# V's columns into the padded tiles: copies on ScalarE in place of transfers, weight pieces behind the fillers

## The chip, the cores and the metric

The kernel runs as one program on one core of a Trainium2 chip. The metric is the device time of one execution in microseconds. A core has TensorE (PE; PEld is its weight load), VectorE (DVE), ScalarE (ACT), GpSimd (POOL) and SyncE (SP), which issues the plain DMAs from one queue, in program order. Each engine runs its own instructions in order and waits for semaphores of the others.

## The reference

Two stages. The first is attention over pooled keys for 8 batches, 8 heads, 576 queries and head size 64: keys and values are averaged over groups of 8, which leaves 72 per head.

```
k_p = k.reshape(B, H, 72, 8, D).mean(axis=3)
v_p = v.reshape(B, H, 72, 8, D).mean(axis=3)
scores = scale * q @ k_p^T ;  scores -= max
attn = exp(scores) / (sum(exp(scores)) + 1e-9)
x = attn @ v_p                      # then (B*S, H*D) = (4608, 512)
```

The second is a top-1 mixture of 8 experts: for each of the 4608 rows the expert with the largest `x @ w_gate`, then `relu(x @ w1[e]) @ w2[e]`, times the gate's probability.

## The kernel before

**Two parts.** The attention part works through 36 units of 128 query rows, all 8 heads at a time. Four units belong to each batch, and one more per pair of batches holds the last 64 rows of both; so units 0 to 3 are batch 0, 4 to 7 batch 1, 8 their remainder, 9 to 12 batch 2 and so on. Each unit also computes the gate's logits, and after every group of units a chain on VectorE (the routing chain) finds each row's expert and place; rows are then scattered to memory by expert. The second part loads blocks of 256 rows of an expert and multiplies them with the expert's weights, which are split into two halves of 16 bits (high and low).

**One unit** (the loop at the end of the attention part). TensorE transposes the probabilities (`u_pt`, tile `pp`), ScalarE casts them to 16 bits (`ph`, L519), VectorE makes the remainder (`pl`, L525), and TensorE forms the weighted sum with V (`u_pv`, L552, tile `po`). VectorE then scales it (`u_nrm`, `ri`, L582 to L590). In between stand the scores of later units (`g_s`, L493), their row minimum (`g_min`) and eight exponentials on ScalarE (`g_exp`, L510), the transposes of later queries (`g_qt`, L470, and their copy L473), and "fillers": pieces of the routing chain and of V's preparation that are taken from a list, up to five behind `u_pv`. A filler's ranking matmul (`rank`, L656) stands in TensorE's order and waits for the routing chain on VectorE (L632, L638, L643, L647).

**V's padded tile.** The 576 pooled rows of a batch (72 for each of 8 heads) lie in 5 chunks of 128 rows, so a chunk holds rows of two or three heads. The weighted sum needs for each chunk and head a block of 72 columns (64 of V, 8 of V times the gate's weights) in which rows of other heads are zero: `VB`, three tiles used in turn, 128 rows x (high, low) x 5 chunks x 3 slots x 74 columns. A batch has 12 such blocks. The compact V columns are in `vc`, made by GpSimd's pooling, ScalarE and VectorE; the last step on VectorE is the filler `value` (L396). Batch 0 is masked by VectorE (`masked`). For batches 1 to 7 the tile is set to zero once, and 12 small transfers from SBUF to SBUF put each head's rows into their block: `value` appends them to the list `moves`, and the loop issues up to 12 of them a unit (units 0 to 3) or 6 (later) on SyncE's queue, behind the unit's other loads (`run(i, "sp")`). One more kind of move, `bd<-bd`, copies a batch's prepared K block to the other half of the partitions.

**Order.** The order is written out by hand: `put(unit, position, function)` places work at a position of a unit, and the loop runs the positions in sequence. Loads of K, V, q and weights stand at position `sp`; ScalarE's high halves of the first expert's weights at `act2`; quarters of three low halves (`lsplit`, L836) at `dve`, which on VectorE lies ahead of the fillers. GpSimd's pooling additions (L330, L332) are made to start behind VectorE's reciprocal of a unit.

Of the kernel before, what the change touches and what calls it, by code (L numbers as in the profile page):

```python
# [12 lines left out]
AF = mybir.ActivationFunctionType  # L13
# [13 lines left out]
HS = (0, 1, 3, 5, 5)  # L27
SLOTS = ((0, 2), (0, 3), (0, 3), (0, 3), (2, 3))
# [3 lines left out]
def kernel(  # L32
# [10 lines left out]
    nc = tc.nc  # L43
    B, H, S, D = q.shape
    N, Dm = out.shape
    E = w1.shape[0]
    F = w1.shape[2]
    KP = S // POOL
# [90 lines left out]
    mk = consts.tile([128, 5, 3], F32, name="mk")  # L139
# [79 lines left out]
    VB = [loads.tile([128, 2, 5, 3, CS], F16, name=f"vb{i}") for i in range(3)]  # L219
# [63 lines left out]
        nc.gpsimd.memset(BD[i], 0.0)  # L283

    def blank(i):
        nc.gpsimd.memset(VB[i] if i else VB[i][:, 1, :, :, 72:73], 0.0)
        nc.gpsimd.tensor_tensor(VB[i][:, 0, :, :, 72:73], mk16[:, :, :, None], z16[:, :, :, None], op=OP.add)

    for i in range(3):
        blank(i)  # L290
# [4 lines left out]
    KVS = {}  # L295
    fillers = []
    moves = []

    TWO = {"away", "best", "onehot", "guard", "value", "<lambda>", "early_int", "early_shift", "again", "again_int"}

    def fill(n=1, one=False):
        while n and fillers and not fillers[0][1] and not (one and fillers[0][2].__name__ in TWO):
            fillers.pop(0)[2]()
            n -= 1
# [8 lines left out]
    def fill_pe():  # L313
        if fillers and fillers[0][1]:
            fillers.pop(0)[2]()
# [78 lines left out]
    def v_dve(b):  # L394
        vp, vc = KVS.pop(("vp", b)), KVS["vc", b]
        nc.vector.scalar_tensor_tensor(vc[:, 1, :, 0:D], vp, SV, vc[:, 0, :, 0:D], op0=OP.mult, op1=OP.subtract)  # L396
# [9 lines left out]
    def u_dve(b):  # L406
        pm, vc = KVS.pop(("pu", b)), KVS["vc", b]
        Z = {}

        def cross():  # L410
            Z["ut"] = work.tile([128, 5, 3, E], F32, name="ut", bufs=1)
            nc.vector.tensor_tensor(Z["ut"], pm[:, 0:120].rearrange("p (c s e) -> p c s e", s=3, e=E),
                                    mk[:, :, :, None].to_broadcast([128, 5, 3, E]), op=OP.mult)

        def gather():
            Z["u"] = pm[:, 128:128 + 5 * E].rearrange("p (c e) -> p c e", e=E)
            nc.vector.tensor_reduce(Z["u"], Z["ut"].rearrange("p c s e -> p c e s"), axis=AX.X, op=OP.add)

        def high():
            nc.vector.tensor_scalar(vc[:, 0, :, D:], Z["u"], SV, None, op0=OP.mult)  # L420

        def low():
            nc.vector.scalar_tensor_tensor(vc[:, 1, :, D:], Z["u"], SV, vc[:, 0, :, D:], op0=OP.mult,
                                           op1=OP.subtract)

        def value():
            v_dve(b)
            if b > 0:
                KVS.pop(("vc", b))
                for c in range(5):  # L430
                    for s in range(*SLOTS[c]):
                        h = HS[c] + s
                        r0, r1 = max(KP * h, 128 * c) - 128 * c, min(KP * h + KP, 128 * c + 128) - 128 * c
                        moves.append((VB[b % 3][r0:r1, :, c, s, 0:D + E], vc[r0:r1, :, c, :], b))

        first = [cross, gather, high, low, value]
        if b < 1:
            first += [lambda: masked(b, 0), lambda: masked(b, 1)]
        fillers[0:0] = [(-1, False, f) for f in first]

    def masked(b, s):
        vc = KVS["vc", b] if s == 0 else KVS.pop(("vc", b))
        nc.vector.tensor_tensor(VB[b][:, s, :, :, 0:D + E], vc[:, s, :, None, :].to_broadcast([128, 5, 3, D + E]),
                                mk16[:, :, :, None].to_broadcast([128, 5, 3, D + E]), op=OP.mult)
# [61 lines left out]
    def g_exp(G, j):  # L506
        ps, nmx, slots = PS_.pop((G, j))
        for x, (h, s) in enumerate(slots):
            p = pbuf[groups[G][s] % 4]
            nc.scalar.activation(p[:, h * KP:(h + 1) * KP], ps[:, x * KP:(x + 1) * KP], AF.Exp,  # L510
                                 bias=nmx[:, x:x + 1], scale=-1.0)

    def u_pt(i):
        p = pbuf[i % 4]
        pp = psA.tile([128, 1024], F32, name="pp")
        for c in range(5):
            nc.tensor.transpose(pp[:, c * 128:(c + 1) * 128], p[:, c * 128:(c + 1) * 128], ident)  # L517
        ph = work.tile([128, 640], F16, name="ph")
        nc.scalar.activation(ph, pp[:, 0:640], AF.Copy, scale=SP)  # L519
        PP_[i] = (pp, ph)  # L520

    def u_lo(i):
        pp, ph = PP_[i]
        pl = work.tile([128, 640], F16, name="pl")
        nc.vector.scalar_tensor_tensor(pl, pp[:, 0:640], SP, ph, op0=OP.mult, op1=OP.subtract)  # L525
        PP_[i] = (ph, pl)

    def u_pv(i):
        b, r = units[i]
        ph, pl = PP_.pop(i)  # L530
        assert all(m[2] > b + (r is None) for m in moves)
        po = psA.tile([128, 2, 512], F32, name="po")
        PO_[i] = po
        first = {}
        for x, y in ((0, 0), (0, 1), (1, 0)):
            a = (ph, pl)[x]
            for c in range(5):
                h0, hend = HS[c] + SLOTS[c][0], HS[c] + SLOTS[c][1]
                while h0 < hend:
                    half = h0 // 4  # L540
                    h1 = min(hend, 4 * half + 4)
                    sl = slice(h0 - HS[c], h1 - HS[c])
                    cols = slice((h0 - 4 * half) * CW, (h1 - 4 * half) * CW)
                    st = first.get(half, True)
                    if r is None:
                        for s in range(2):
                            nc.tensor.matmul(po[64 * s:64 * s + 64, half, cols],
                                             a[:, c * 128 + 64 * s:c * 128 + 64 * s + 64],
                                             VB[(b + s) % 3][:, y, c, sl, 0:CW], start=st, stop=False,
                                             skip_group_check=True)  # L550
                    else:
                        nc.tensor.matmul(po[:, half, cols], a[:, c * 128:(c + 1) * 128],  # L552
                                         VB[b % 3][:, y, c, sl, 0:CW], start=st, stop=False, skip_group_check=True)
                    first[half] = False
                    h0 = h1
# [39 lines left out]
    def flush(n=99, upto=99):  # L595
        while n and pend and pend[0][0] <= upto:
            _, f, u = pend.pop(0)
            f(u)
            n -= 1
# [147 lines left out]
    for c in (4, 2, 3, 0, 1):  # L747
        n = 128 if c < 4 else 64
# [41 lines left out]
    def put(i, pos, f, *a):  # L790
        assert 0 <= i < NU
        hooks.setdefault((i, pos), []).append((f, a))
# [14 lines left out]
    for g in range(NPAIR):  # L807
        u0 = 9 * g
        e, o = 2 * g, 2 * g + 1
        if g:  # L810
            for b, at, last in ((e, u0 - 11, u0 - 8), (o, u0 - 7, u0 - 3)):
                first = 1 if (g == 1 and b == e) else 0
                for f, x in ((pool_k, 0), (pool_v, 2)):
                    for y in range(2):
                        put(POOLAT[b] + x + y, "q", f, b, y)
                    n = 2 * b + x // 2 + 3
# [24 lines left out]
        put(at, "q", wsplit, 0, j, "p", 0, on_beat)  # L841
    for j, at in ((1, 15), (3, 23), (4, 27)):
        for x in range(4):
            put(at + x, "dve", lsplit, j, x, 4)

    def pass_ids(g, i, h, j):
        nc.gpsimd.tensor_tensor(g, h, zf.to_broadcast([128, 2]), op=OP.add)
# [69 lines left out]
    def run(i, pos):  # L917
        for f, a in hooks.pop((i, pos), []):
            f(*a)

    def routes(i):
        gidx, u = GOF[i]
        if u == bounds[gidx][1] - 1:
            return route(gidx)
# [34 lines left out]
    for i in range(NU):  # L959
        A, Z = halves.get(2 * i), halves.get(2 * i + 1)  # L960
        Y = halves.get(2 * i - 1)
        if i < 30 and aged:
            flush(1)
            run(i, "q")
        else:
            run(i, "q")
            flush(1)
        u_pt(i)
        if A:
            g_s(*A)  # L970
        if Y:
            g_exp(*Y)
        if i in turns:
            g_qt(*turns[i])
        if (i, "pe") not in hooks:
            fill_pe()
        run(i, "pe")
        u_lo(i)
        if A:
            g_min(*A)  # L980
            g_exp(*A)
        run(i, "act")
        run(i, "dve")
        u_pv(i)
        fill(5 if i < 30 else 4)
        run(i, "pe2")
        fill_pe()
        run(i, "sp")
        for _ in range(min(12 if i < 4 else 6, len(moves))):
            nc.sync.dma_start(*moves.pop(0)[:2])  # L990
        if Z:
            g_s(*Z)
        aged = len(pend)
        u_nrm(i, (lambda: g_min(*Z)) if Z else None)
        run(i, "act2")
        run(i, "dve2")
        last = routes(i)
        fill(3 if i >= NU - 3 else 2, POOLAT[2] < i < 30)
# [323 lines left out]
```

## Time and profile before

| | us |
|---|---|
| median of 3 runs | 646.71 (644.49 to 648.65) |
| profiled execution, its own time | 643.21 |
| its span, first to last instruction | 641.4 |
| busy: TensorE, VectorE, ScalarE, GpSimd | 582.9, 324.4, 279.9, 266.9 |
| mean granted TensorE clock | 0.946 |

The profile is of one execution that was not among the three timed ones. Busy time of an engine counts overlapping instructions once. The granted clock is told as a share of 2.4 GHz; 0.50 is the 1.2 GHz level.

### The profile page before, as it was taken

The numbers are of one execution on the slowest core, as the hardware profiler recorded it, in microseconds if no ns is written. First come the engines' busy times: TensorE is split into PE (matmuls) and PEld (weight loads), VectorE is DVE, ScalarE is ACT, GpSimd is POOL, SyncE is SP. The second block draws the span as 40 slices with busy tenths as digits, with TensorE's granted clock in tenths as the row PEclk, the third lists the DMA queues.
The fourth block names the chain that finished last, engine by engine and source line by source line (L and its number), as shares of the span: only waits on it lengthen the run. The fifth ranks groups of instructions, "written<-read, shape, count | busy, mean of one in ns | idle before, by whom it ended". The sixth has DMA issues, their size and how long they took to land. (4 is left out here: it accounts for less than half of the span.)

```text
span 641.4 us, 15846 instructions
## 1 busy us (share of the span) xinstructions
PE 582.9 (91%) x4631; PEld 432.6 (67%) x4632; DVE 324.4 (51%) x736; ACT 279.9 (44%) x628; POOL 266.9 (42%) x477
## 2 busy tenths in 40 slices
PE   6897869789868989899999999999999999999983
PEld 4796758779767746666776667677667677667661
DVE  5565929967788664512551122146122731273672
ACT  1584829865766323421542222235222721262671
POOL 7583828677886351320432111223203132214264
PEclk7597969977879999999999999999999999999998
DMA  8974787886725469496467222334823283318310
GB/s 249 301 259 108 212 243 213 248 245 189 222 79 116 165 168 329 116 411 210 98 208 250 65 49 66 98 79 128 306 52 87 58 306 111 93 33 299 75 42 11
DMA packets 105417, 105.78 MB, mean 165 GB/s; under 512 B 63523, under 2 KB 73763, under 8 KB 105381
## 3 DMA queue, kind: packets, MB, share of 16 engines
q1 hardware_dynamic: 98740, 85.62, 47.6%
q0 software_dynamic: 6640, 19.71, 8.2%
q8 instruction: 18, 0.29, 0.2%
q14 instruction: 19, 0.15, 0.1%
HBM read 71.77 MB, written 22.06 MB: 146 GB/s over the span
## 5 line engine op out<-in xcount | busy, mean ns | idle before, releaser
L1020 PEld LDWEIGHTS <-bd 128*128 128x128 f16 x936 | 91.1, 98 | 108.7 <-DVE bd L1014 2.2
L1014 DVE SCALAR_TENSOR_TENSOR bd<-ps,bd 128x512 f16<-128x512 f32 (+1 forms) x44 | 27.4, 630 | 145.3 <-ACT bd L1010 127.6
L1230 POOL TENSOR_TENSOR spacer<-ql,iG 1x1 f32<-1x1 f32 x44 | 17.9, 406 | 165.9 <-ACT ql L1226 151.8
L510 ACT ACTIVATE both<-ps,nmx 128x72 f32<-128x72 f32 x288 | 68.6, 326 | 9.0 <-DVE nmx L503 8.7
L1020 PE MATMUL po<-kv,bd 128*128 128x512 f16 x264 | 59.0, 379 | 2.5 <-ACT bd L1010 1.8
L1020 PE MATMUL po<-w,bd 128*128 128x512 f16 x264 | 59.1, 379 | 0.0
L493 PE MATMUL ps<-bd,qT 128*128 128x144 f32 x256 | 53.4, 342 | 5.3 <-DMA bd<-bd 3.9
L1231 POOL DMA_INDIRECT out_dram<-ql,iG x44 | 48.5, 1102 | 21.7 <-issue 20.0
L1010 ACT ACTIVATE bd<-ps 128x512 f16<-128x512 f32 (+1 forms) x44 | 23.8, 547 | 67.2 <-PE L946 33.4
L330 POOL TENSOR_TENSOR st<-kv 128x1280 f32<-128x1280 f32 x14 | 40.9, 2921 | 22.7 <-DVE ri L583 14.6
L1020 PE MATMUL pq<-kv,bd 128*128 128x512 f16 x216 | 48.1, 379 | 0.0
L493 PEld LDWEIGHTS ps<-bd,qT 128*128 128x128 f32 x256 | 42.8, 228 | 6.9 <-issue 4.3
L519 ACT ACTIVATE ph<-pp 128x640 f16<-128x640 f32 x36 | 25.4, 704 | 49.8 <-PE pp L517 47.4
L552 PE MATMUL po<-vb,ph 128*128 128x146 f16 (+2 forms) x384 | 34.8, 241 | 12.6 <-DMA vb<-vc 7.9
L685 POOL DMA_INDIRECT x_by_expert<-both,rpos x36 | 35.5, 987 | 25.4 <-DVE both L681 5.5
L946 PE MATMUL ps<-kv,w 128*128 128x256 f16 (+1 forms) x176 | 43.1, 258 | 3.3 <-ACT kv L111 2.0
L948 PE MATMUL ps<-kv,qt 128*128 128x256 f16 (+1 forms) x176 | 44.8, 263 | 1.0 <-DVE qt L113 1.0
L946 PE MATMUL ps<-kv,qt 128*128 128x256 f16 (+1 forms) x176 | 44.8, 263 | 0.0
L947 PE MATMUL ps<-kv,qt 128*128 128x256 f16 (+1 forms) x176 | 44.8, 263 | 0.0
L948 PE MATMUL ps<-kv,w 128*128 128x256 f16 (+1 forms) x176 | 43.1, 258 | 0.0
L947 PE MATMUL ps<-kv,w 128*128 128x256 f16 (+1 forms) x176 | 43.1, 258 | 0.0
L1020 PE MATMUL pq<-w,bd 128*128 128x512 f16 x192 | 42.7, 379 | 0.0
(250 smaller groups left out, 1354.8 us busy)
## 6 DMA issues: line engine op xcount, KB each, us to landing
st<-in_moe_w_dram SPq DMA_DIRECT2D x8, 2048.0 KB
both<-in_moe_w_dram SPq DMA_DIRECT2D x6, 2048.0 KB, 10.4
vb<-x_by_expert SPq DMA_DIRECT2D x16, 514.0 KB
kv<-in_k_dram SPq DMA_DIRECT2D x7, 1024.0 KB
kv<-in_v_dram SPq DMA_DIRECT2D x7, 1024.0 KB
qt<-in_q_dram SPq DMA_DIRECT2D x6, 1024.0 KB
st<-in_moe_w_dram SPq DMA_DIRECT2D x4, 1024.0 KB
qt<-in_q_dram SPq DMA_DIRECT2D x4, 512.0 KB
```

The source lines that it names most:

```text
L330: on_beat(nc.gpsimd.tensor_tensor(t1, src[:, :, 0:4 * D], src[:, :, 4 * D:], op=OP.add))
L493: nc.tensor.matmul(ps[:, x * 2 * KP:(x + 1) * 2 * KP], t[:, h, :], BD[b % 3][:, :, h, :], start=True, stop=True)
L510: nc.scalar.activation(p[:, h * KP:(h + 1) * KP], ps[:, x * KP:(x + 1) * KP], AF.Exp, bias=nmx[:, x:x + 1], scale=-1.0)
L519: nc.scalar.activation(ph, pp[:, 0:640], AF.Copy, scale=SP)
L552: nc.tensor.matmul(po[:, half, cols], a[:, c * 128:(c + 1) * 128], VB[b % 3][:, y, c, sl, 0:CW], start=st, stop=False, skip_group_check=True)
L685: st = nc.gpsimd.indirect_dma_start(out=xs, out_offset=bass.IndirectOffsetOnAxis(ap=Z["pos"][:, u:u + 1], axis=0), in_=X[:, u, :], in_offs ...
L946: nc.tensor.matmul(dst, wh, xT[:, d, 0:n], start=(d == 0), stop=False)
L947: nc.tensor.matmul(dst, wh, xT[:, DC + d, 0:n], start=False, stop=False)
L948: nc.tensor.matmul(dst, wl, xT[:, d, 0:n], start=False, stop=(d == DC - 1))
L1014: V.scalar_tensor_tensor(l, p, 0.0, h, op0=OP.max, op1=OP.subtract)
L1020: nc.tensor.matmul(y, hT[x][:, f, 128 * j:128 * j + 128], W2[s][z][:, f, :], start=(half == x == z == f == 0), stop=(half == z == 1 and f ...
L1231: st = nc.gpsimd.indirect_dma_start(out=out, out_offset=bass.IndirectOffsetOnAxis(ap=iG[:, j:j + 1], axis=0), in_=ys[j], in_offset=None, b ...
```

## The change

Batches 1 to 7: the 12 transfers of a batch are gone. In their place ScalarE copies whole 128-row blocks of `vc` into the padded tile, each scaled by a column of `mk` that is one in the head's rows and zero in the others (`place`). `value` lists the 12 blocks, and the loop issues up to 6 copies (units 0 to 3) or 4 (later) a unit, behind `act2`. Since the copies write the zeros too, only one column of the tiles is still cleared at the start. The moves that are left (`bd<-bd`) are issued as soon as they are listed. The quarters of the weights' low halves go to a new position `dve3`, behind the fillers.

```diff
     def blank(i):
-        nc.gpsimd.memset(VB[i] if i else VB[i][:, 1, :, :, 72:73], 0.0)
+        nc.gpsimd.memset(VB[i][:, 1, :, :, 72:73], 0.0)
...
         def value():
             v_dve(b)
             if b > 0:
-                KVS.pop(("vc", b))
-                for c in range(5):
-                    for s in range(*SLOTS[c]):
-                        h = HS[c] + s
-                        r0, r1 = max(KP * h, 128 * c) - 128 * c, min(KP * h + KP, 128 * c + 128) - 128 * c
-                        moves.append((VB[b % 3][r0:r1, :, c, s, 0:D + E], vc[r0:r1, :, c, :], b))
+                places.extend((b, c, s) for c in range(5) for s in range(*SLOTS[c]))
...
+    def place(n):
+        for b, c, s in places[:n]:
+            nc.scalar.activation(VB[b % 3][:, :, c, s, 0:D + E], KVS["vc", b][:, :, c, :], AF.Copy,
+                                 scale=mk[:, c, s:s + 1])
+        del places[:n]
...
     for j, at in ((1, 15), (3, 23), (4, 27)):
         for x in range(4):
-            put(at + x, "dve", lsplit, j, x, 4)
+            put(at + x, "dve3", lsplit, j, x, 4)
...
         fill(5 if i < 30 else 4)
+        run(i, "dve3")
         run(i, "pe2")
         fill_pe()
         run(i, "sp")
-        for _ in range(min(12 if i < 4 else 6, len(moves))):
+        for _ in range(len(moves)):
             nc.sync.dma_start(*moves.pop(0)[:2])
...
         run(i, "act2")
+        place(6 if i < 4 else 4)
         run(i, "dve2")
```

ScalarE's order in units 2 and 3, behind the copy of batch 2's K block (`bd_171`); `vb_173` is batch 1's padded tile. Before:

```order
L368 ACTIVATE bd_171<-pq 64x512
L519 ACTIVATE ph<-pp 128x640
L510 ACTIVATE both<-ps,nmx 128x72 x4
L473 ACTIVATE qT<-pq 128x512
L510 ACTIVATE both<-ps,nmx 128x72 x4
```

And now (lines behind the edit are numbered two or three higher):

```order
L369 ACTIVATE bd_171<-pq 64x512
L439 ACTIVATE vb_173<-vc,mk 128x2x72 x6
L521 ACTIVATE ph<-pp 128x640
L512 ACTIVATE both<-ps,nmx 128x72 x4
L475 ACTIVATE qT<-pq 128x512
L512 ACTIVATE both<-ps,nmx 128x72 x4
L439 ACTIVATE vb_173<-vc,mk 128x2x72 x6
```

Six copies stand ahead of unit 3's cast `ph`, and six more ahead of unit 4's.

SyncE's queue in units 7 to 9: `vb_174` is batch 2's padded tile, `bd_169` batch 3's K block, `st_64` a weight load. Before:

```order
L990 DMA vb_174<-vc 24x2x72
L990 DMA vb_174<-vc 48x2x72
L990 DMA vb_174<-vc 72x2x72
L990 DMA vb_174<-vc 8x2x72
L990 DMA vb_174<-vc 64x2x72
L247 DMA kv_163<-in_k_dram 64x512
L250 DMA kv_163<-in_k_dram 128x4x512
L990 DMA bd_169<-bd_169 64x576
L99 DMA st_64<-in_moe_w_dram 128x2x1024
```

And now:

```order
L254 DMA qt_166<-in_q_dram 128x8x256
L247 DMA kv_150<-in_v_dram 64x512
L250 DMA kv_150<-in_v_dram 128x4x512
L247 DMA kv_163<-in_k_dram 64x512
L250 DMA kv_163<-in_k_dram 128x4x512
L993 DMA bd_169<-bd_169 64x576
L99 DMA st_64<-in_moe_w_dram 128x2x1024
```

The K load and the block's copy directly follow the loads of q and V; the small transfers are gone.

VectorE's order in unit 16, from the remainder `pl` on; `w_01_61<-st_64` is the weight piece, `ra`, `req`, `rm`, `oh` the routing chain. Before:

```order
L525 SCALAR_TENSOR_TENSOR pl<-pp,ph 128x640
L503 TENSOR_REDUCE nmx<-ps 128x4
L836 SCALAR_TENSOR_TENSOR w_01_61<-st_64,w_00_60 128x256
L632 TENSOR_TENSOR ra<-L,rm 128x32
L638 SCALAR_TENSOR_TENSOR req<-ra,down 128x32
L643 TENSOR_REDUCE rm_1797<-req 128x4
L647 TENSOR_TENSOR oh<-req,rm_1797 128x32
L582 TENSOR_SCALAR ri<-po 128x8
```

And now:

```order
L527 SCALAR_TENSOR_TENSOR pl<-pp,ph 128x640
L505 TENSOR_REDUCE nmx<-ps 128x4
L634 TENSOR_TENSOR ra<-L,rm 128x32
L640 SCALAR_TENSOR_TENSOR req<-ra,down 128x32
L645 TENSOR_REDUCE rm_1796<-req 128x4
L649 TENSOR_TENSOR oh<-req,rm_1796 128x32
L838 SCALAR_TENSOR_TENSOR w_01_61<-st_64,w_00_60 128x256
L584 TENSOR_SCALAR ri<-po 128x8
```

The piece has moved from ahead of the routing chain to behind it, still ahead of the scaling. Units 24 and 28 have the same picture.

## Rows read from the trace of the kernel before

**Rows 1.** Stretches (us): length, busy PE, PEld, DVE, ACT, POOL, clock, DMA share, GB/s.

```profile
0.00:219.40 219.40, 178.81 (x1621) 159.07 (x1623) 155.37 (x480) 129.74 (x421) 146.72 (x177) 0.85 0.72 207
219.40:641.40 422.00, 404.13 (x3013) 273.53 (x3010) 169.07 (x257) 150.17 (x207) 120.17 (x300) 0.99 0.48 143
54.00:58.00 4.00, 3.22 (x24) 2.84 (x24) 1.09 (x4) 0.00 (x0) 0.61 (x1) 0.50 0.61 150
76.00:96.00 20.00, 12.42 (x88) 11.13 (x87) 8.11 (x29) 6.37 (x21) 7.54 (x8) 0.74 0.90 264
126.00:136.00 10.00, 8.19 (x50) 7.83 (x51) 5.92 (x19) 5.04 (x16) 3.40 (x3) 0.66 0.95 278
```

**Rows 2.** Waits, 30 to 219.4 us: who for whom, total us, times, longest.

```profile
ACT ph L519 <- PE pp L517: 47.4, 26, 7.0
...
PE po L552 <- DMA vb<-vc: 7.9, 6, 2.0
...
PE ps L493 <- DMA bd<-bd: 3.9, 1, 3.9
...
ACT w L111 <- DMA st<-in_moe_w_dram: 1.8, 1, 1.8
```

**Rows 3.** TensorE's timeline in unit 4: start, us, instruction, [idle before].

```profile
51.98 0.24 PE L552 MATMUL po<-vb,ph 128*128 128x146 f16 x1 [1.46 <-DMA vb<-vc]
54.18 0.34 PE L552 MATMUL po<-vb,ph 128*128 128x219 f16 x1 [1.96 <-DMA vb<-vc]
55.12 0.95 PE L552 MATMUL po<-vb,ph 128*128 128x73 f16 x7 [0.60 <-DMA vb<-vc]
```

**Rows 4.** SyncE's timeline, 38 to 122 us: issues.

```profile
44.02 9.80 SPq L990 DMA_DIRECT2D vb<-vc  x12
...
80.78 0.51 SPq L990 DMA_DIRECT2D bd<-bd  x1
...
114.92 4.93 SPq L990 DMA_DIRECT2D vb<-vc  x6
119.94 0.54 SPq L254 DMA_DIRECT2D qt<-in_q_dram  x1
```

**Rows 5.** TensorE's timeline, units 9, 10 and 18.

```profile
80.68 0.30 PE L552 MATMUL po<-vb,ph 128*128 128x146 f16 x1 [2.03 <-DMA vb<-vc]
82.59 1.16 PE L552 MATMUL po<-vb,ph 128*128 128x219 f16 x8 [1.61 <-DMA vb<-vc]
...
85.39 1.27 PE L517 MATMUL pp<-ident,both 128*128 128x128 f32 x5
90.60 1.30 PE L493 MATMUL ps<-bd,qT 128*128 128x144 f32 x4 [3.94 <-DMA bd<-bd]
...
127.81 1.02 PE L470 MATMUL pq<-ident,qt 128*128 128x128 f32 x4 [1.96 <-DMA qt<-in_q_dram]
```

**Rows 6.** ScalarE's groups, 30 to 219.4 us: count, busy us, mean ns, idle before.

```profile
L510 ACT ACTIVATE both<-ps,nmx 128x72 f32<-128x72 f32 x271 | 64.7, 326 | 4.3 <-DVE nmx L503 4.0
...
L111 ACT ACTIVATE w<-st 128x1024 f16<-128x1024 f32 x8 | 8.6, 1072 | 1.8 <-DMA st<-in_moe_w_dram 1.8
...
L392 ACT ACTIVATE vc<-vp 128x320 f16<-128x320 f32 x7 | 3.3, 474 | 0.0
```

**Rows 7.** ScalarE's timeline in units 3 and 4.

```profile
45.05 0.70 ACT L519 ACTIVATE ph<-pp 128x640 f16<-128x640 f32 x1 [0.51 <-PE pp L517]
45.65 0.95 ACT L510 ACTIVATE both<-ps,nmx 128x72 f32<-128x72 f32 x4
...
48.45 0.70 ACT L519 ACTIVATE ph<-pp 128x640 f16<-128x640 f32 x1 [0.48 <-PE pp L517]
```

**Rows 8.** VectorE's timeline in units 16 and 20.

```profile
118.35 1.20 DVE L836 SCALAR_TENSOR_TENSOR w<-st,w 128x256 f16<-128x256 f32 x1
...
140.38 2.81 DVE L632 TENSOR_TENSOR ra<-L,rm 128x32 f32<-128x32 f32 x1
```

**Rows 9.** GpSimd's timeline in unit 20.

```profile
140.22 2.90 POOL L330 TENSOR_TENSOR st<-kv 128x1280 f32<-128x1280 f32 x1
```

More of the change, by code (lines that the diff above doesn't have):

```diff
@@ L297 @@
     moves = []
+    places = []
     TWO = {"away", "best", "onehot", "guard", "value", "<lambda>", "early_int", "early_shift", "again", "again_int"}
@@ L530, in u_pv @@
         ph, pl = PP_.pop(i)
-        assert all(m[2] > b + (r is None) for m in moves)
+        assert all(x > b + (r is None) for x, *_ in places) and all(m[2] > b + (r is None) for m in moves)
         po = psA.tile([128, 2, 512], F32, name="po")
```

## The prediction, made before the result was known

> **What bounds the kernel now.** I read the busy time by stage first [rows 1]. Up to 219.4 us, where the last attention unit ends, TensorE is busy for 178.8 us at a mean granted clock of 0.85; the 422 us behind it run at 0.99 with 404 us busy. The edit touches only the first part, and what it moves in the second begins a little earlier or later as a whole, so all terms below are of these 219 us. The list of waits [rows 2] says who holds the first part up. ScalarE waits 47.4 us, over 26 units, for TensorE's transposes: it is not the bound as a whole. TensorE waits 7.9 us for the small transfers that write V into the padded tile, 3.9 us for the copy of K's block, and ScalarE once 1.8 us for a weight load.
>
> Then the single places. In unit 4 the weighted sum stops for 1.46, 1.96 and 0.60 us, each time for the next small transfer [rows 3]. The SyncE timeline shows why [rows 4]: the twelve transfers of batch 1 could not start before 44.02, took 9.80 us to issue (0.82 us each), and stood in front of everything else. In unit 9 the same wait is 2.03 and 1.61 us [rows 5], and 3.94 us follow for K's block of batch 3, whose copy was issued only at 80.78 [rows 4, 5]. In unit 18 the transposes wait 1.96 us for a q load that was issued at 119.94, right behind six small transfers begun at 114.92 [rows 4, 5].
>
> A stop costs more than itself: after the stops in unit 4 the granted clock is 0.50, the 1.2 GHz level, at 54 to 58 us; it is 0.74 over 76 to 96 and 0.66 over 126 to 136 [rows 1]. Each time one of these stops stood just ahead of it.
>
> **The change, term by term**, against the profiled execution's own 643.2 us.
>
> *Unit 4.* The waits end: 7.9 less 3.64 of unit 9 is 4.3 us [rows 2, 5]. TensorE then runs some 4 us of the path at half clock, which costs 2.0 us. Gain 6.3; bounds 4.3 (the clock falls anyway) and 6.3.
>
> *Unit 9.* 2.03 and 1.61 are 3.64 us. From 82.59 to the end of the transposes at 85.39 + 1.27 = 86.66, 4.1 us are run at the low level: 2.0 more. Gain 5.6, bounds 3.6 and 5.6.
>
> *Unit 10, K's block.* In SyncE's order six small transfers disappear ahead of the K load and the block copy, so the load can be issued when its buffer is free and the copy when ScalarE has written the block (unit 8), about 6 us earlier than 80.78. The copy then has only that load in front of it; but TensorE arrives 5 us earlier too, and DMA is already busy for 0.90 of 76 to 96 us [rows 1]. Bounds 0 and 3.94 + 2.0 of low clock = 5.9. I take 5.0, nearer to the upper end, because q's load and the load of V issue before the copy and land in the stretch that is now spent on issuing.
>
> *Unit 18.* The q load is in SyncE's program at unit 15; without the six transfers before it (4.93 us) it issues 5 us earlier, against a wait of 1.96. With the clock, (1 − 0.66) × 10 = 3.4 us, the upper bound is 5.4, the lower 0. VectorE has dense work in this unit, so I take 4.0.
>
> *The weight load.* SyncE had twelve transfers around it; ScalarE's 1.8 us for it [rows 2] should go. Bounds 0 and 1.8; taken 1.8.
>
> *ScalarE's copies.* 84 copies of 128 x 144 are new, a shape and operand pattern that no row shows together. Below: four exponentials with a column as operand take 0.95 us [rows 7] and one alone 0.326 [rows 6], so they follow each other at (0.95 − 0.326) / 3 = 0.21 us; 72 more elements at (1072 − 474) / (1024 − 320) = 0.85 ns [rows 6] add 0.06. One copy every 0.27 us: 84 × 0.27 = 22.7 us, 3.2 per batch. Above: if copies did not overlap, the 0.326 us of the exponential [rows 6] plus 0.06 is 0.39 us, 33 in all. I take 22.7, as the exponentials do overlap. The Trainium skill (ScalarE: Activation LUTs, What ACT_TABLE_LOAD costs) gives 186 ns + 0.833 ns an element, 93 ns more for a pointer operand, and an overlap of 93 ns: an estimate of 0.31 us a copy, 25.7 us in all, by which the exposed part below would be 9 us rather than 8.
>
> What of it is exposed is a matter of the unit's pace. A plain unit takes 48.45 − 45.05 = 3.40 us, and ScalarE is idle for 0.48 of them [rows 7]; four copies need 1.07, six 1.6. So units 2 and 3 lose about 1.1 each (2.2), and the next three batches, placed beside units of about this pace, 3.2 less three times 0.5, that is about 1.5 each (4.5). The last three lie in units that other work stretches to 5 to 9 us: 0.5 each (1.5). Behind the copies on ScalarE stands the cast of the next unit's probabilities, for which VectorE's low part and the weighted sum wait. Cost 8; bounds 0 (all in the 47.4 us of waiting) and 33 (all exposed).
>
> *Weight pieces behind the fillers.* In units 16, 24 and 28 a piece stood before the routing chain on which the ranking matmul waits; the longest shown here took 1.20 us [rows 8]. If that came back in each of the three units, the gain would be 3.6. But the routing chain's own first subtraction took 2.81 us in unit 20 without a piece before it, while GpSimd's addition ran from 140.22 to 143.12 [rows 8, 9], so the wait can pass from the piece to the subtraction. Gain 0.5, bounds 0 and 3.6. The Trainium skill (SBUF — State Buffer, Who interferes with whom) says that a VectorE instruction with two SBUF inputs contends with a GpSimd instruction that reads SBUF and that the later one blocks; piece and subtraction both have two. By it the term is near 0, without it 3.6; the 2.81 us agrees with it.
>
> *The rest.* The smaller memsets lie beside the first loads: nothing; without that cover they would still be a gain. SyncE's later waits and the landing of small transfers leave with them.
>
> *What is late next.* VectorE and GpSimd: when units follow more closely, GpSimd's additions meet VectorE's chain more often. I charge one more stop like the 2.81 us.
>
> Sum: −(6.3 + 5.6 + 5.0 + 4.0 + 1.8 + 0.5) + 8 + 2.8 = −12.4. Against 643.2 that is 630.8; the three timed runs before have a median of 646.7, 3.5 above the profiled execution, and 646.7 − 12.4 = 634.3. I forecast **633 us**.
>
> **Rivals.**
>
> *The waits only change their name.* K's block still comes late, because the loads that issue earlier fill the queue in front of it (DMA busy 0.90 in 76 to 96 speaks for that), and the copies are exposed for 12 us. Then 6.3 + 5.6 + 2.0 + 1.8 − 12 − 2.8 leaves 1 us: about 646, no change. Against it: the queue moved little while SyncE was issuing, 0.61 at 54 to 58.
>
> *ScalarE becomes the bound.* Its place is the cast at the head of each of the 20 units with copies. It decides once four copies cost more than the idle 0.48 us and nothing later in the unit absorbs the rest: at 0.39 us each, 33 us exposed less 23.2 gained is 10 us slower, 656. For it speaks that the exponentials already fill most of the 3.40 us; against it that they overlap, and that ScalarE waits 47.4 us for TensorE. The Trainium skill (ScalarE: Activation LUTs, Rules for kernel authors) advises VectorE rather than ScalarE for simple elementwise work, which fits this case; here VectorE has no room either (unit 16 is dense with it).
>
> *More comes back than I count.* The upper bounds of all gains, 28.6, and a cost of 5 give 646.7 − 23.6 = 623.
>
> That the change does something else is excluded: the orders show 84 copies on ScalarE and none of the small transfers left on SyncE.
>
> **Chances.** The forecast (626 to 641) 0.62, waits that change their name (641 to 651) 0.19, ScalarE as the bound 0.09, more than counted 0.10. About 1%, 6.5 us, is what a measurement of this kernel can tell from no change, and the forecast's lower edge touches it: faster 0.74, same 0.17, slower 0.09. The range runs from 623 (all upper bounds) to 645 (the first rival taken in nearly whole).
>
> **What would show it.** In the profile of the changed kernel: no wait of the weighted sum for a DMA in units 4 and 9, and a granted clock near 1.00 at the places that now show 0.50; K's block landed before unit 10 asks for it; the q load of unit 18 issued 5 us or more ahead; copies one every 0.27 us; TensorE's waits for the cast longer than now, by 8 us in all; the attention stage over at about 207 us, and the part behind it as long as before. I am wrong if the stage ends after 215 us: then either the block copy or the copies' exposure is what I mis-sized.

## The result, and the profile after

The changed kernel takes **620.5 us** (median of 4 runs, 619.44 to 622.84) where the kernel before, run beside it, takes 647.68 (4 runs, 644.49 to 648.7): ratio 0.9623, 95% interval 0.9558 to 0.9687. On another chip it was 620.53 against 643.81, ratio 0.9632 (0.959 to 0.9674). The forecast was 633, so the sign was right and the gain about twice the forecast; the time lies 2.5 us below the range (623 to 645), and below the 623 of the third rival. The profiled execution took 622.84 us, span 618.7, mean granted clock 0.967.

By stretch (columns as in [rows 1]), the changed kernel's attention stage now ends at 197.1 us (start of the last unit's scaling on VectorE; 219.2 before), 22.1 earlier; the part behind it is as long as before, 421.4 against 422.0. The last three are units 3 and 4, 8 to 12, and 17 and 18:

```profile
0.00:197.30 197.30, 167.08 (x1624) 147.49 (x1626) 148.99 (x480) 152.72 (x505) 143.91 (x177) 0.91 0.76 224
197.30:618.70 421.40, 404.08 (x3009) 273.07 (x3007) 169.36 (x257) 150.06 (x207) 118.90 (x300) 0.99 0.48 143
50.00:54.00 4.00, 2.79 (x35) 2.18 (x33) 2.73 (x11) 4.00 (x16) 2.13 (x1) 1.00 0.00 0
72.00:92.00 20.00, 18.30 (x185) 16.83 (x184) 16.11 (x56) 19.12 (x66) 17.10 (x18) 1.00 0.87 256
108.00:118.00 10.00, 9.27 (x109) 8.56 (x107) 9.26 (x33) 9.11 (x28) 7.60 (x8) 1.00 1.03 316
```

The places that ran at a granted clock of 0.50, 0.74 and 0.66 run at 1.00. DMA is as busy as before (0.87 to 1.03): the transfers that stay did not have to become fewer.

The list of waits, 24 to 197.3 us (who for whom, total us, times, longest), answers to [rows 2]. No wait of TensorE for a DMA is left; ScalarE's wait for the transposes fell from 47.4 to 11.9:

```profile
DVE pl L527 <- ACT ph L521: 17.6, 22, 1.4
...
ACT ph L521 <- PE pp L519: 11.9, 12, 2.4
...
PE po L554 <- ACT ph L521: 7.9, 10, 1.2
...
PE pq L658 <- DVE oh L649: 6.2, 8, 2.0
```

TensorE's timeline in units 4, 9, 10 and 18 answers to [rows 3, 5]. The weighted sums run through, the scores of unit 10 (79.47) and the transposes of unit 18 (112.19) wait for nothing; what is left in unit 4 is 0.65 us for the cast behind the copies and 0.57 for the routing chain:

```profile
51.84 0.96 PE L554 MATMUL po<-vb,ph 128*128 128x146 f16 x12 [0.65 <-ACT ph L521]
52.70 0.57 PE L554 MATMUL po<-vb,pl 128*128 128x146 f16 x6
53.84 0.19 PE L658 MATMUL pq<-oh,before 128*128 128x32 f16 x1 [0.57 <-DVE oh L649]
...
74.29 0.96 PE L554 MATMUL po<-vb,ph 128*128 128x146 f16 x12
...
79.47 0.73 PE L495 MATMUL ps<-bd,qT 128*128 128x144 f32 x4
...
112.19 0.60 PE L472 MATMUL pq<-ident,qt 128*128 128x128 f32 x4
```

SyncE's timeline (issues) answers to [rows 4]:

```profile
62.57 0.58 SPq L250 DMA_DIRECT2D kv<-in_k_dram  x1
71.55 0.48 SPq L993 DMA_DIRECT2D bd<-bd  x1
...
92.87 0.70 SPq L254 DMA_DIRECT2D qt<-in_q_dram  x1
```

The copy of K's block for unit 10 is issued at 71.55 instead of 80.78, and the load in front of it left 9 us before; the q load of unit 18 is issued 27 us earlier, at 92.87, so SyncE now runs several units ahead.

ScalarE's timeline in units 2 and 3, and the group of all copies (columns as in [rows 6]):

```profile
44.66 1.93 ACT L439 ACTIVATE vb<-vc,mk 128x144 f16<-128x144 f16 x6
46.49 0.69 ACT L521 ACTIVATE ph<-pp 128x640 f16<-128x640 f32 x1
...
49.26 1.94 ACT L439 ACTIVATE vb<-vc,mk 128x144 f16<-128x144 f16 x6
51.09 0.70 ACT L521 ACTIVATE ph<-pp 128x640 f16<-128x640 f32 x1
...
L439 ACT ACTIVATE vb<-vc,mk 128x144 f16<-128x144 f16 x84 | 27.9, 418 | 1.7 <-DVE ri L584 1.5
```

Alone a copy is 0.418 us; six take 1.94, so one follows another every (1.94 − 0.418) / 5 = 0.305 us.

### The profile page after: what moved, and what is told of

The parts are those of the page before. It is cut to its first block, busy times and chain, and to the rows that moved or that the text cites. A ratio compares the mean times of both kernels' runs of the same rounds, so it can differ in the third digit from the quotient of the medians.

```text
span 618.7 us, 15764 instructions
## 1 busy us (share of the span) xinstructions
PE 571.2 (92%) x4631; PEld 420.6 (68%) x4632; DVE 318.4 (51%) x736; ACT 302.8 (49%) x712; POOL 262.8 (42%) x477
## 5 line engine op out<-in xcount | busy, mean ns | idle before, releaser
L1234 POOL TENSOR_TENSOR spacer<-ql,iG 1x1 f32<-1x1 f32 x44 | 19.6, 446 | 165.8 <-ACT ql L1230 151.7
L495 PE MATMUL ps<-bd,qT 128*128 128x144 f32 x256 | 49.4, 322 | 1.4 <-ACT bd L754 1.4
L554 PE MATMUL po<-vb,ph 128*128 128x146 f16 (+2 forms) x384 | 31.2, 230 | 11.9 <-ACT ph L521 7.9
L495 PEld LDWEIGHTS ps<-bd,qT 128*128 128x128 f32 x256 | 39.4, 212 | 2.5 <-ACT bd L754 1.8
L1230 ACT ACTIVATE ql<-po,gB 128x512 f32<-128x512 f32 x22 | 15.1, 685 | 51.4 <-PE L948 39.5
```

Source lines behind the costliest of these rows:

```text
L495: nc.tensor.matmul(ps[:, x * 2 * KP:(x + 1) * 2 * KP], t[:, h, :], BD[b % 3][:, :, h, :], start=True, stop=True)
```

## The experiments

"After" means the changed kernel. The time of a unit is the distance from the start of its cast to the start of the next one.

**The two halves apart.**

```diff
-            put(at + x, "dve3", lsplit, j, x, 4)
+            put(at + x, "dve", lsplit, j, x, 4)
```

> The changed kernel with the weight pieces back ahead of the fillers; all else as changed (620.5 us). My theory: the second half of the change is worth little, 0.5 to 1.5 us, so this runs at 621 to 622.5; the shorter VectorE times in the changed profile (routing subtractions and pieces together 10.3 us against 18.8) come from GpSimd's additions starting at another phase of the unit. Rival: they come from the order of the pieces; then 4 us or more are given back, 624.5 and above, and the stops of units 16, 24 and 28 return.

Measured: 619.62 us (618.26 to 620.84), ratio 0.9639 (0.9607 to 0.9672): no difference from after. VectorE's twelve pieces of one tile group (L838: count; ns min/median/max), first after, then this run:

```profile
L838 DVE SCALAR_TENSOR_TENSOR w<-st,w x12: 394/416/1925, 101.5 to 176.1; 128x256 f16<-128x256 f32 x12
```

```profile
L838 DVE SCALAR_TENSOR_TENSOR w<-st,w x12: 413/642/2147, 100.9 to 175.1; 128x256 f16<-128x256 f32 x12
```

In sum the pieces take 11.5 us here and 6.6 after, the ten routing subtractions 1.8 here and 3.7 after. Units 16 and 18 are 0.3 and 1.0 us longer, and from unit 24 on the differences are hardly larger than between two runs of the changed kernel (the last experiment). The wait lands on whichever of the two comes first, and with four copies a unit the position of the pieces is worth nothing that could be measured.

**The queue apart from the consumer.** V still comes by copies, but the 84 small transfers go out again at their old places, into a buffer that nobody reads.

```diff
                 places.extend((b, c, s) for c in range(5) for s in range(*SLOTS[c]))
+                spare = W2[0][1][:, 6:8, :].rearrange("p c x -> p (c x)")
+                for n, (_, c, s) in enumerate(places[-12:]):
...
+                    moves.append((dst, KVS["vc", b][r0:r1, :, c, :], 99))
...
-        for _ in range(len(moves)):
+        for _ in range(min(12 if i < 4 else 6, len(moves))):
```

> The changed kernel, and beside the copies the 84 small transfers are issued again on SyncE's queue at their old places, into an idle buffer that nobody reads. Theory: about half of the gain is the queue that was blocked (K's block in unit 10, the q load of unit 18, the V load behind unit 20's stop, the weight load), so 8 to 14 us are given back: 629 to 635, with waits for bd or q loads in units 10 and 18, and none of the weighted sum for a DMA. Rival: only the weighted sum's own wait for the transfers counted; then at most 2 us are given back, 620 to 623.

Measured: 637.47 us (635.61 to 638.34), ratio 0.9914 (0.9877 to 0.9951): 17 us given back, more than either theory had. Units 1 to 5, 7 to 9 and 11 to 17 are as long as after, to 0.07 us. The loss stands in a few stops: units 6 and 10 (K's block, 4.2 and 3.2 us longer), 18 to 20 (5.9), 23 (a weight load, 3.2) and 33 (a transposing transfer of rows for the second part, 4.1). TensorE's timeline of this run, with VectorE and GpSimd in unit 20, and then SyncE's waits for `vc` in this run and in the kernel before (who for whom, total us, times, longest):

```profile
63.54 1.15 PE L501 MATMUL ps<-bd,qT 128*128 128x144 f32 x4 [3.22 <-DMA bd<-bd]
...
84.24 1.30 PE L501 MATMUL ps<-bd,qT 128*128 128x144 f32 x4 [2.83 <-DMA bd<-bd]
...
122.92 0.66 PE L478 MATMUL pq<-ident,qt 128*128 128x128 f32 x4 [2.65 <-DMA qt<-in_q_dram]
...
135.16 3.37 DVE L655 TENSOR_TENSOR oh<-req,rm 128x32 f16<-128x32 f32 x1
...
135.57 2.90 POOL L331 TENSOR_TENSOR st<-kv 128x1280 f32<-128x1280 f32 x1
```

```profile
SPq L999 <- DVE vc L397: 30.7, 7, 7.8
...
SPq L990 <- DVE vc L396: 27.0, 5, 7.3
```

So transfers that nobody waits for cost 17 us, through the loads behind them. In unit 20 an instruction of the routing chain is held up by GpSimd's addition again, as before the change (8.5 us for the unit, 5.0 after). SyncE loses time at these transfers in two ways: it issues each in 0.8 us, and it first stands still until `vc` is written, 30.7 us in all here. How the 17 us divide between the two was not tested. A queue that stands still costs nothing by that alone: in the changed kernel it stands 64.1 us for ScalarE ahead of block copies, and TensorE waits for no DMA.

**Are the transfers themselves dear, or their place in the queue?** The same 84 transfers, three a unit and behind the K blocks. (The buffer is part of a weight tile that is filled meanwhile, so some of one expert's low weight halves are overwritten.)

```diff
-                    moves.append((dst, KVS["vc", b][r0:r1, :, c, :], 99))
+                    idle.append((dst, KVS["vc", b][r0:r1, :, c, :]))
...
+        for _ in range(min(3, len(idle))):
+            nc.sync.dma_start(*idle.pop(0))
```

> The changed kernel with the same 84 small transfers into an idle buffer, but issued three a unit, behind that unit's loads and behind the copies of the K blocks, where the earlier run with them issued twelve or six in a row. Theory (what costs is the row of transfers in front of a load or a block's copy, 5 to 10 us of issuing): of the 18 us that the row gave back, most goes away; this run is 0 to 5 us slower than the changed kernel, and the stops for K blocks in units 6 and 10 and for the q load in unit 18 are under 1 us each. Rival (the transfers themselves cost, by the DMA engines' time or by blocked SBUF ports, however they are queued): 12 us or more slower than the changed kernel, and VectorE's or the loads' own durations longer all over the stage.

Measured: 628.79 us (627.62 to 630.07), ratio 0.9756 (0.9714 to 0.9799): 8.3 us slower than after, between the two. But 6.7 of them are unit 10 and 1.6 unit 18; units 1 to 9, beside which 21 of the transfers were issued, and 11 to 17 are as long as after to 0.06 us. SyncE's and TensorE's rows of unit 10:

```profile
70.11 0.56 SPq L247 DMA_DIRECT2D kv<-in_k_dram  x1
73.98 0.37 SPq L250 DMA_DIRECT2D kv<-in_k_dram  x1
74.47 0.53 SPq L1000 DMA_DIRECT2D bd<-bd  x1
...
83.09 1.30 PE L502 MATMUL ps<-bd,qT 128*128 128x144 f32 x4 [5.67 <-DMA bd<-bd]
```

Six transfers in a row (64.33 to 69.97) stood before the K load at 70.11; its larger part (1 MB) then waited 3.3 us more for the V load to land and was issued at 73.98, right in front of the block copy, which TensorE still waits for at 83.09. After has 9 us between the two. The rival falls: beside units 1 to 9 and 11 to 17 the transfers cost neither ports nor landing time that a unit's length shows. The theory's size was wrong since even a short row can push one load in front of a block that is needed at once. SyncE also stands less for `vc` here, 10.7 us against 30.7, so this run doesn't tell the row's issuing from the standing either.

**The price of the copies.** Every copy twice.

```diff
-            nc.scalar.activation(VB[b % 3][:, :, c, s, 0:D + E], KVS["vc", b][:, :, c, :], AF.Copy,
-                                 scale=mk[:, c, s:s + 1])
+            for _ in range(2):
+                nc.scalar.activation(VB[b % 3][:, :, c, s, 0:D + E], KVS["vc", b][:, :, c, :], AF.Copy,
+                                     scale=mk[:, c, s:s + 1])
```

> Every copy is issued twice: 84 more at the 0.305 us at which they follow each other in the changed profile, 25.6 us more of ScalarE. Theory: in units with copies ScalarE is already what ends a unit, so nearly all of the second set is exposed: 16 to 25 us slower, 636 to 645. Rival: ScalarE still has slack in the stage; then under 8 us, below 628.5.

Measured: 653.64 us (652.88 to 654.85), ratio 1.0163 (1.0117 to 1.0209): 33 us slower than after. A unit with four more copies is 1.8 us longer, though four at 0.305 would be 1.22; six cost 2.7 against 1.83. ScalarE's rows show why, first this run (with a stretch, columns as in [rows 1]), then after:

```profile
70.97 3.12 ACT L440 ACTIVATE vb<-vc,mk 128x144 f16<-128x144 f16 x8
...
48.00:75.00 27.00, 17.89 (x169) 15.70 (x170) 14.72 (x50) 25.58 (x83) 12.77 (x10) 0.92 0.54 164
```

```profile
63.29 1.33 ACT L439 ACTIVATE vb<-vc,mk 128x144 f16<-128x144 f16 x4
```

Eight copies take 3.12 us and four 1.33, which is 1.8 apart. A second copy into the same block starts 0.438 us behind the first on average (so they do not overlap), and the next block's 0.32 behind that. A doubled copy thus adds 0.45 us and not 0.305, 38 us in all, of which 33 appear in the time: the theory that nearly all is exposed holds, and its price was too low. ScalarE is busy for 25.58 of 27 us, so it sets the pace; the lower clock (0.92) is not needed to explain the length of a unit.

**Cheaper copies.** The scale a constant.

```diff
-                                 scale=mk[:, c, s:s + 1])
+                                 scale=1.0)
```

> The copies are scaled by the constant 1 instead of a column of ones and zeros, so the masking of other heads' rows is left out; shape and number stay. This prices the column operand. Theory: a copy follows the next at about 0.21 us instead of 0.305, 8 us less of ScalarE, of which 3 to 6 come back: 614.5 to 617.5. Rival: what copies cost is handed back by VectorE's routing chain, which otherwise waits for GpSimd's addition; then under 2 us come back (618.5 or more), and the subtractions of the routing chain get longer in the profile.

Measured: 628.41 us (626.33 to 631.73), ratio 0.9774 (0.9723 to 0.9825); the second part has other rows per expert here and is longer (431.8 us), so only the stage is compared: it ends at 193.4, 3.7 us earlier, but 2.2 of these are a wait in front of the last unit's scaling, which the run with the pieces ahead lacks too, with the copies as changed. Units 1 to 17 are 2.7 us shorter in sum and units 18 to 23 2.1 longer, and the last cast starts at 190.48 against 191.99 and 189.57 in the two profiles of after. So under 2 us come back by the copies, as the rival had it. A copy takes 328 ns (median), 0.09 less than with a column as operand. Units with copies are 0.35 to 0.55 us shorter, but units 8, 12, 16 and 20 are 0.7, 0.3, 0.5 and 3.0 us longer. Unit 20 shows why, VectorE's and GpSimd's rows:

```profile
120.91 3.63 DVE L648 TENSOR_TENSOR oh<-req,rm 128x32 f16<-128x32 f32 x1
...
121.58 2.90 POOL L331 TENSOR_TENSOR st<-kv 128x1280 f32<-128x1280 f32 x1
```

The small two-input instruction of the routing chain ends at 124.54, the addition at 124.48. Where units get shorter, VectorE's chain runs into GpSimd's addition, and most of the gain goes back.

**Three copies a unit**, in place of four from unit 4 on, alone and with the pieces ahead of the fillers.

```diff
-        place(6 if i < 4 else 4)
+        place(6 if i < 4 else 3)
```

> The changed kernel with three copies a unit in place of four from unit 4 on, so that a batch's 12 copies lie in four units and not in three. By the copies' own price: four copies are 1.22 us against 0.48 us of idle ScalarE, so 0.74 us a unit and 2.2 a batch is exposed; three are 0.92, so 0.44 a unit and 1.75 a batch; six batches save 2.7 us: 2 to 3 us faster than the changed kernel. Rival (the routing subtraction takes it back, as in the run with a plain scale: units with shorter copies let GpSimd's addition run into it): no difference, within 1.5 us, and subtractions and weight pieces that are longer in all by 2 us or more.

> Three copies a unit and the weight pieces back ahead of the fillers. If the two edits are independent, this is 2 to 3 us faster than the changed kernel by the copies and 0 to 1 us by the pieces, so 616 to 619 where the changed kernel takes 620.5. If what is blocked by GpSimd's addition is only the next VectorE instruction with two inputs, whichever it is, the sum of subtractions and pieces stays at 10 to 14 us and the time within 1.5 us of the changed kernel.

Measured: 621.37 us (619.49 to 621.68), ratio 0.963 (0.9588 to 0.9672), and 624.43 (623.29 to 625.96), ratio 0.9688 (0.9646 to 0.9731): no difference, and 3.9 us slower. In the first, most units that had four copies gain some 0.3 us as expected, and units 8, 12 and 16 lose 0.59, 0.92 and 0.43. These three now hold three copies each, which was charged at 0.44, and their subtractions take 0.79, 0.80 and 0.58 us instead of 0.18 each; subtractions and pieces together are 13.8 us against 10.3. That is what the rival named, but the loss of these units is not split between copies and subtractions. For the second neither theory holds: subtractions and pieces take 16.5 us, and beside three copies a unit the pieces' old place costs 3.1 us (624.43 against 621.37). There VectorE and GpSimd at unit 30 stand like this, with TensorE's stop behind it:

```profile
170.77 2.13 DVE L838 SCALAR_TENSOR_TENSOR w<-st,w 128x256 f16<-128x256 f32 x1
...
173.08 1.78 DVE L680 TENSOR_SCALAR res<-res 128x4 f32<-128x4 f32 x1
...
170.72 1.90 POOL L864 TENSOR_TENSOR bd<-vb,zf 128x1024 f16<-128x1024 f32 x1
172.70 2.13 POOL L865 TENSOR_TENSOR bd<-vb,bd 128x1024 f16<-128x1024 f32 x1
...
176.36 0.94 PE L554 MATMUL po<-vb,ph 128*128 128x146 f16 x12 [2.31 <-DVE l L589]
```

A piece of 0.41 us takes 2.13, and a multiplication of 128x4 takes 1.78 and ends at 174.86 with the addition (174.83). The unit is 3.4 us longer than in the profile after, 2.9 than in the second one.

**Copies on VectorE**, all of them, and every second one.

```diff
-            nc.scalar.activation(VB[b % 3][:, :, c, s, 0:D + E], KVS["vc", b][:, :, c, :], AF.Copy,
-                                 scale=mk[:, c, s:s + 1])
+            nc.vector.tensor_scalar(VB[b % 3][:, :, c, s, 0:D + E], KVS["vc", b][:, :, c, :],
+                                    mk[:, c, s:s + 1], None, op0=OP.mult)
```

> The changed kernel with the 84 copies on VectorE (one multiplication by the same column of ones and zeros each) at the same place of the unit. In a unit with four copies VectorE now idles 1.04 us before the remainder, waiting for ScalarE's cast. If a copy takes VectorE 0.1 to 0.2 us, four fit into that idle time, the units that lost 0.6 to 1.2 us to the copies go back to 3.4 us, and the kernel gains most of their 7.8 us: 613 to 616. Rival (the copies are one more thing that GpSimd blocks: they stand about 1.9 us behind the reciprocal, and GpSimd's addition starts 0.9 us behind it and runs 2.9 us): in units 3, 7, 11, 15, where an addition runs, the first copy takes 1 us or more, the routing subtraction loses the room that the longer units gave it, and the kernel is no faster than the changed one, 619 to 626.

> Every second copy on VectorE, the others on ScalarE. Two copies are 0.61 us of ScalarE, against the 0.48 that it has idle, so nearly nothing of them is exposed. Theory of the free time on both engines: 613 to 616. Rival (VectorE's copies wait for GpSimd, and shorter units let the addition run into the routing subtraction): 618 to 624, with subtractions and pieces of 9 us or more in all.

Measured: 645.22 us (642.38 to 649.29) against 641.12 before on this chip, ratio 1.0056 (1.0027 to 1.0085), 24.7 us slower than after; with half of them 629.04 (627.35 to 632.47), ratio 0.9823 (0.9787 to 0.9859). The collision that both rivals named is there, at a price far above what they gave. It hits the copies alone: the routing subtractions of the first run take 0.18 us each, where its rival expected them longer. VectorE, GpSimd and the waits of the first:

```profile
75.47 1.73 DVE L439 TENSOR_SCALAR vb<-vc,mk 128x144 f16<-128x144 f16 x1
...
74.25 2.90 POOL L331 TENSOR_TENSOR st<-kv 128x1280 f32<-128x1280 f32 x1 [0.93 <-DVE ri L585]
...
PE po L554 <- DVE pl L527: 30.2, 17, 5.1
```

The first copy of the unit ends at 77.20, the addition at 77.15. A copy that meets no addition takes 0.25 us; 31 of the 84 take over 0.3, up to 2.49, and all 84 take 54.5 us. The remainder `pl` stands behind them, and the weighted sum behind that. ScalarE's copies, at 0.42 us, were never held up: their longest is 0.47.

**After again**, beside the runs above.

> The changed kernel itself, on the same chip as the three kernels beside it. Expected again 0.96 of the time before (0.956 to 0.968). A ratio above 0.975 would mean that the gain depends on the chip.

Measured: 620.53 us (619.35 to 621.8), ratio 0.9632 (0.959 to 0.9674). Its units 1 to 17 are as long as in the first profile to 0.02 us; units 24 to 30 differ by up to 1.1 each and 1.6 in sum, so smaller differences there are not read in any run.

None of these versions beats the changed kernel beyond the scatter.

## Why the forecast had the sign right and the size wrong

| term of the sum | forecast, us | measured in the two profiles, us |
|---|---|---|
| unit 4 | −6.3 | −6.5 (10.81 to 4.27) |
| unit 9 | −5.6 | −5.3 (9.96 to 4.66) |
| unit 10, K's block | −5.0 | −4.9 (9.39 to 4.46) |
| unit 18, q load | −4.0 | −3.3 (9.03 to 5.72) |
| weight load (unit 23) | −1.8 | −0.8 (5.72 to 4.96) |
| ScalarE's copies | +8 | +7.3 (units 2, 3, 6, 7, 11, 13, 15, 19, 22 alone) |
| pieces behind the fillers | −0.5 | 0 (the first experiment) |
| what is late next | +2.8 | −7.4 (units 8, 16, 20, 21) |
| units 30, 31 and small rests | 0 | −1.2 |
| sum | −12.4 | −22.1 |

*The waits that end* were sized rightly, stop and clock together. The first rival, waits that change their name, fell: K's block came in time, not because DMA had room (it is as busy), but because the K load left 9 us ahead. (The share of 0.61 that the prediction read against this rival is of the loads issued from 53.94 on; while the twelve transfers were issued, at 44 to 54 us, it was 0.13.) *The q load* was right in sign, and 27 us earlier instead of 5, for SyncE's whole program moved forward.

*ScalarE's copies* are close to the charge only as the table books them: eleven of the twenty units that hold copies stand in other rows, which are net of them. A plain unit takes 3.40 us (unit 31) and one with four copies 4.0 (units 7, 11, 14, 22); at 0.6 in each of the eighteen such units and 1.2 in units 2 and 3 the copies would cost 13 us, an estimate, and the gains in the other rows would be some 6 us larger than they stand there. A copy follows the next every 0.305 us instead of 0.27; besides, 3.2 less 1.5 is 1.7 a batch, where the prediction charged 1.5. TensorE's waits for the cast rose from 1.4 to 7.9 us. The Trainium skill (ScalarE: Activation LUTs, What ACT_TABLE_LOAD costs) gives 186 ns + 0.833 ns an element, 93 ns for a pointer operand and an overlap of 93 ns. By that a copy is 0.399 us long and follows every 0.306; the trace shows 0.418 and 0.305, and 0.09 less without the pointer. Here the page was nearer than my interpolation. The rival of ScalarE as the bound holds inside the units with copies, where ScalarE is busy for 4.00 of 4.00 us (50 to 54) and 19.12 of 20 (72 to 92), but not at its price of 33 us.

*Weight pieces*: near 0, for the reason given; the wait passes between piece and subtraction.

**What failed is the step "What is late next".** I charged one more stop of 2.8 us, arguing that units that follow more closely let GpSimd's additions meet VectorE's chain more often. The opposite happened. Before, VectorE and GpSimd in unit 8, then GpSimd, TensorE and unit 21's weighted sums around unit 20:

```profile
73.01 1.55 DVE L632 TENSOR_TENSOR ra<-L,rm 128x32 f32<-128x32 f32 x1
...
71.59 2.90 POOL L330 TENSOR_TENSOR st<-kv 128x1280 f32<-128x1280 f32 x1
...
132.44 2.89 POOL L330 TENSOR_TENSOR st<-kv 128x1280 f32<-128x1280 f32 x1 [7.98 <-DMA kv<-in_v_dram]
...
143.91 0.19 PE L656 MATMUL pq<-oh,before 128*128 128x32 f16 x1 [2.79 <-DVE req L638]
...
148.53 1.65 PE L552 MATMUL po<-vb,ph 128*128 128x146 f16 x12
```

In unit 8 the subtraction took 1.55 us beside an addition, 0.18 now. In unit 16 it was the piece, 1.20 us [rows 8] beside an addition until 119.25, now 0.42. For unit 20 the V load, issued behind the small transfers, held GpSimd for 7.98 us; so its next addition came in the middle of unit 20 and blocked the subtraction [rows 8, 9]. TensorE stopped for 2.79 us, and unit 21 still ran at the low level (granted clock 0.50 at 146 to 150, 1.65 us for 12 weighted sums). After, in the same unit, GpSimd and VectorE:

```profile
121.12 2.91 POOL L331 TENSOR_TENSOR st<-kv 128x1280 f32<-128x1280 f32 x1
...
124.18 0.18 DVE L634 TENSOR_TENSOR ra<-L,rm 128x32 f32<-128x32 f32 x1
```

The addition starts 0.84 us behind VectorE's reciprocal (120.28) and ends at 124.03, 0.15 us before the subtraction. Two reasons can be told apart by runs. One is the queue: with the idle transfers back, units 20 and 21 are 13.6 us together, against 14.1 before and 9.7 now, while units 8 and 16 stay short. There GpSimd waited for VectorE and not for the V load, so that it was this load is read from the trace before alone. The other, in units 8 and 16, is the copies themselves: a unit of 4.0 to 4.5 us instead of 3.4 leaves room for 2.9 us of addition. Shorter copies (the constant scale, three a unit) take that room away: the subtractions of units 8, 12 and 16 rise from 0.18 us each to 0.92, 0.91, 0.68 and to 0.79, 0.80, 0.58. In these two ways units 8, 16, 20 and 21 became 7.4 us shorter, and from the 2.8 that I charged that is 10.2 apart; the sum missed by 9.7. That the other terms add up so nearly is in part luck, since the cost of the copies is spread over them. I had read both rows, but as a fixed nuisance to be counted, where the time of the addition hangs on the load that the change sets free. The Trainium skill (SBUF — State Buffer, Who interferes with whom) says that the one that issues later blocks wholly; the pairs in the rows above agree, all but two, in which VectorE's `oh` began first (120.91 against 121.58, 135.16 against 135.57). Its rule names the pair and not which of them is late.

The third rival gave 623, but by upper bounds of the gains, which were not what came back.

Of the 27.2 us by medians the two profiled executions show 20.4 in their own times (643.21 and 622.84) and 22.7 in their spans: before was profiled 4.5 us below the median of the runs beside it, after 2.3 above. The medians on the second chip differ by 23.3, so the 27.2 is the largest reading of the gain.

## What to carry to other kernels

A row of small transfers on one queue costs through the load behind it, not by itself: look for the transfers that nobody waits for, and ask which load stands next. When a change frees a load, follow its consumer to the next engine that it blocks: a wait in the profile can be moved or ended by a transfer that isn't named in it. A cheaper engine for a copy is not the faster one if a neighbour can hold it up: VectorE's copy of 0.25 us cost more than ScalarE's of 0.42.

## What the runs showed of the hardware that was not expected

- Small instructions of VectorE that met a GpSimd addition ended with it, within 0.1 us, with one tensor input too: a multiplication of 128x4 took 1.78 us, a copy of 128x144 2.49 at most, against 0.25 alone. The 128x256 weight piece ended 0.28 us behind its addition (172.90 against 172.62).
- Two instructions of the routing chain that began 0.67 and 0.41 us ahead of an addition were held until its end as well (120.91 in the run with a constant scale, 135.16 in the one with idle transfers). Both began while GpSimd issued a scatter (120.57 to 121.56, 134.54 to 135.54); whether that held them first was not tested.
- Two ScalarE copies into the same block started 0.438 us apart on average, two into different blocks 0.305 (0.32 in the run with every copy twice).
- The 21 small transfers beside units 1 to 9 moved no unit by more than 0.06 us, though SyncE took 0.8 us to issue each.
- A stop of TensorE costs more than itself: the stops in unit 4 were 4.0 us in sum, and the unit, which holds no copies, is 6.5 us shorter without them; 54 to 58 us had run at a granted clock of 0.50.
